# Transposing the first two row tiles before their 1/std is known, with the scale applied when V leaves PSUM

## The chip, the cores and the metric

The kernel runs on one core of one Trainium2 chip. The metric is the device time of one launch in microseconds (us). Before the change the median of 4 runs is 693.38 us (693.23 to 695.09).

## The reference

x is 2048 rows of 1024 numbers in bf16. One transformer block is computed: attention with a causal window of 256 on a layer norm of x, then a feed-forward part with SiLU on a layer norm of the result. The layer norms have no learned scale or shift. What matters here is the head of it:

```
def _layernorm(x, axis=-1, eps=1e-5):
    m = jnp.mean(x, axis=axis, keepdims=True)
    v = jnp.var(x, axis=axis, keepdims=True)
    return (x - m) / jnp.sqrt(v + eps)
...
qkv = (x @ wqkv) ... ; q, k, v = qkv[0], qkv[1], qkv[2]
h  = x + _A_ref(_layernorm(x, axis=-1), A_wqkv, A_wo)
h2 = h + _B_ref(_layernorm(h, axis=-1), B_w1, B_w2)
```

Each row of V is (row of x − mean) / std times the V columns of wqkv. The division by std is one number for each row, so it can be done before the product or after it.

## The kernel before

The 2048 rows are 4 blocks of 512, and each block is 4 row tiles of 128 rows. A product needs the normed rows transposed, so that the 1024 columns lie on the 128 partitions in 8 slices (kt 0 to 7). `lnT_b[0]` holds the transposed block 0: 8 slices by 512 rows.

Block 0 is the start of the program, when nothing else can run yet. Its V product has 8 groups: row tile j (0 to 3) by column half c (0, 1). `v_group(0, j, c)` is 8 matmuls of 128x512 (one for each kt) into one bank of PSUM (the matmul's output memory), and a copy of that bank into `v`. The matmuls have line L245 and the copy L247. The Q and K products of block 0 follow (`qk_group`, L255, copied by L257), which need all four row tiles of `lnT_b[0]`. Two banks take turns for these groups (`acc_banks`, `next_acc`).

The order of the work is written by hand: each engine's queue holds its instructions in the order in which the program emits them, and an instruction that waits holds up those behind it on the same engine. The order on each queue before the change:

- SP's queue issues loads: x tile 0, the first half of the V weights (`load_wqkv(2 * D)`, 1 MB, L139), x tile 2, the second half of the V weights, x tile 3, and the first Q weights. Tile 1 is issued from ScalarE's queue. Later come one DMA transpose (`ln_transpose`, L198) for tile 3, three more weight loads, and the four x tiles of block 1.
- TensorE (PE) first runs 11 matmuls on zeros to be warm (L162). Tiles 0, 1 and 2 are transposed on PE (`turn_first`, two 128x128 transposes at a time, L223) and copied from PSUM to `lnT_b[0]` by ScalarE (L224). Tile 3 goes through the DMA transpose.
- The layer norm of a tile: VectorE (DVE) reads it twice for statistics (`ln_half`, L166, then L174), ScalarE takes the root (`ln_root`, L201), DVE the reciprocal (L208) and the norm itself (`ln_norm`, L194). For tiles 0 and 1 the norm is done in quarters inside `ln_first`, one quarter of tile 0 on ScalarE (L217).
- V groups run in the order (j, c) = (0,0), (1,0), (0,1), (1,1), (2,0), (2,1), (3,0), (3,1).

During block 0's 16 Q and K groups, the layer norm of block 1 is given out as 16 steps (4 statistics, 4 steps of 1/std, 4 norms, 4 DMA transposes), none after each of the first 4 groups, one after each of the next 6, and two after each later one. Block 1's V product starts after them, with the first attention scores of block 0 (L360) in front. The odd groups among the 16 are copied out by DVE, the even ones by ScalarE.

Of the kernel before, what the change touches and what calls it, by code (L numbers as in the profile page):

```python
# [9 lines left out]
F32 = mybir.dt.float32  # L10
I32 = mybir.dt.int32
ACT = mybir.ActivationFunctionType
ALU = mybir.AluOpType

P = 128
# [29 lines left out]
def kernel(  # L45
# [10 lines left out]
    nc = tc.nc  # L56
# [3 lines left out]
    S, D = x2d.shape  # L60
# [4 lines left out]
    KT = D // P  # L65
# [4 lines left out]
    scale = float(DH) ** -0.5  # L70

    const = ctx.enter_context(tc.tile_pool(name="const", bufs=1))
    small = ctx.enter_context(tc.tile_pool(name="small", bufs=2))
# [12 lines left out]
    r_e = big.tile([P, 13312], BF16, name="r_e")  # L86
# [4 lines left out]
    tp_ps = [tp_pool.tile([P, 1024], BF16, name=f"tp{i}") for i in range(4)]  # L91
    o_ps = [ps.tile([P, 8, 64], F32, name=f"o_ps{i}") for i in range(2)]
    acc_ps = [ps.tile([P, 512], F32, name=f"acc{i}") for i in range(2)]

    def view(region, off, *dims):
        n = 1
        for d in dims:
            n *= d
        ap = region[:, off:off + n]
        if len(dims) == 2:  # L100
            return ap.rearrange("p (a b) -> p a b", b=dims[1])
        if len(dims) == 3:
            return ap.rearrange("p (a b c) -> p a b c", b=dims[1], c=dims[2])
        return ap
# [4 lines left out]
    lnT_b = [view(r_w, 24576, KT, 512), view(r_t, 0, KT, 512)]  # L109
    x_ring = [view(r_o, i * 1024, 1024) for i in range(8)]  # L110
# [17 lines left out]
    wqkv_v = A_wqkv.rearrange("(kt p) n -> p kt n", p=P)  # L128
# [5 lines left out]
    def load_x(b, j, queue=nc.sync):  # L134
        queue.dma_start(out=x_ring[(b % 2) * 4 + j], in_=x2d[(b * 4 + j) * P:(b * 4 + j + 1) * P, :])  # L135

    def load_wqkv(c0):
        dst = wqk[:, :, c0:c0 + 512] if c0 < 2 * D else wv[:, :, c0 - 2 * D:c0 - 2 * D + 512]
        nc.sync.dma_start(out=dst, in_=wqkv_v[:, :, c0:c0 + 512])  # L139

    eps = const.tile([P, 1], F32, name="eps")
    nc.vector.memset(eps[:], LN_EPS)
# [1 line left out]
    nc.scalar.activation(out=dummy[:], in_=eps[:], func=ACT.Sqrt)  # L144

    load_x(0, 0)
    load_wqkv(2 * D)
    load_x(0, 1, nc.scalar)
    load_x(0, 2)
    load_wqkv(2 * D + 512)  # L150
    load_x(0, 3)
    load_wqkv(0)

    ident = const.tile([P, P], BF16, name="ident")
    make_identity(nc, ident[:])
    warm = view(r_e, 0, 2, 512)
    nc.vector.memset(warm, 0.0)
    nc.gpsimd.memset(v[:, :, :, DH:VW], 1.0)


    for i in range(11):
        nc.tensor.matmul(o_ps[i % 2][:].rearrange("p a b -> p (a b)"), lhsT=warm[:, 0, 0:P], rhs=warm[:, 0, :], start=True, stop=True)  # L162


    def ln_half(xt, stats, c):
        nc.vector.bn_stats(out=stats[:, c, :], in_=xt[:, c * 512:(c + 1) * 512])  # L166

    def ln_stats(xt, st, j, half_done=None):
        stats = half_done
        if stats is None:  # L170
            stats = small.tile([P, 2, 6], F32, name="ln_st", tag="ln_st")
            ln_half(xt, stats, 0)
        ln_half(xt, stats, 1)
        nc.vector.bn_aggr(out=st[:, j, :], in_=stats[:])  # L174
# [18 lines left out]
    def ln_norm(xt, st, rs, j):  # L193
        nc.vector.tensor_scalar(out=xt, in0=xt, scalar1=st[:, j, 0:1], scalar2=rs[:, j:j + 1],  # L194
                                op0=ALU.subtract, op1=ALU.mult)

    def ln_transpose(xt, dst, j):
        nc.sync.dma_start_transpose(out=dst[:, :, j * P:(j + 1) * P], in_=xt)  # L198

    def ln_root(st, rs, j):  # L200
        nc.scalar.activation(out=rs[:, j:j + 1], in_=st[:, j, 1:2], func=ACT.Sqrt, bias=eps[:], scale=1.0)  # L201

    def ln_first(xt, st, rs, j, parts, on_act=0):

        if on_act:
            shift = small.tile([P, 2], F32, name="ln_shift", tag="ln_shift")
            nc.scalar.activation(out=shift[:, 0:1], in_=st[:, j, 0:1], func=ACT.Identity, scale=-1.0)
        nc.vector.reciprocal(out=rs[:, j:j + 1], in_=rs[:, j:j + 1])  # L208
        if on_act:
            nc.scalar.activation(out=shift[:, 1:2], in_=shift[:, 0:1], func=ACT.Identity, scale=rs[:, j:j + 1])  # L210
        n = 1024 // parts
        for h in range(parts):
            part = xt[:, h * n:(h + 1) * n]
            if h < parts - on_act:
                ln_norm(part, st, rs, j)
            else:
                nc.scalar.activation(out=part, in_=part, func=ACT.Identity, bias=shift[:, 1:2], scale=rs[:, j:j + 1])  # L217

    def turn_first(j, h):

        for i in range(2):
            kt = h * 2 + i
            nc.tensor.transpose(out=tp_ps[h][:, i * P:(i + 1) * P], in_=x_ring[j][:, kt * P:(kt + 1) * P], identity=ident[:])  # L223
        nc.scalar.copy(out=lnT_b[0][:, h * 2:(h + 1) * 2, j * P:(j + 1) * P],  # L224
                       in_=tp_ps[h][:, 0:256].rearrange("p (k q) -> p k q", q=P))

    def ln_tiles(tag):
        st = small.tile([P, 4, 2], F32, name=f"st_{tag}", tag=f"st_{tag}")
        rs = small.tile([P, 4], F32, name=f"rs_{tag}", tag=f"rs_{tag}")
        return st, rs  # L230
# [3 lines left out]
    acc_banks = list(a[:] for a in acc_ps)  # L234

    def next_acc():
        acc_n[0] += 1
        return acc_banks[acc_n[0] % len(acc_banks)]

    def v_group(b, j, c, copy, between=None):  # L240
        acc = next_acc()
        for kt in range(KT):
            if between:
                between(kt)
            nc.tensor.matmul(acc, lhsT=lnT_b[b % 2][:, kt, j * P:(j + 1) * P], rhs=wv[:, kt, c * 512:(c + 1) * 512],  # L245
                             start=(kt == 0), stop=(kt == KT - 1))
        copy(out=v[:, b * 4 + j, c * 16:(c + 1) * 16, 0:DH], in_=acc.rearrange("p (h d) -> p h d", d=DH))  # L247
# [172 lines left out]
    class Stream:  # L420
# [18 lines left out]
        def between(self, kt):  # L439
            if self.seen * self.n >= self.done * 192:  # L440
                self.bursts[self.done]()
                self.done += 1
            if self.seen * self.n * 2 >= (self.given * 2 + 1) * 192:
                if pending:
                    pending.pop(0)()
                coming.append(self.pieces[self.given])
                if len(coming) > self.behind:
                    pending.append(coming.pop(0))
                self.given += 1
            self.seen += 1  # L450

    dve, act = nc.vector.tensor_copy, nc.scalar.copy


    st, rs = ln_tiles("a")
    half = small.tile([P, 2, 6], F32, name="ln_st", tag="ln_st")
    ln_stats(x_ring[0], st, 0)
    ln_root(st, rs, 0)
    ln_half(x_ring[1], half, 0)
    ln_first(x_ring[0], st, rs, 0, 4, 1)  # L460
    ln_stats(x_ring[1], st, 1, half)
    for h in range(4):
        turn_first(0, h)
        if h == 2:
            ln_root(st, rs, 1)
    ln_first(x_ring[1], st, rs, 1, 4)
    ln_stats(x_ring[2], st, 2)

    held = []

    def turn_1(kt):
        if kt == 7:
            turn_first(1, 0)

    def turn_1_rest(kt):
        if kt == 2:
            turn_first(1, 3)
            act(**held.pop())
            ln_root(st, rs, 2)

    v_group(0, 0, 0, lambda **args: held.append(args), turn_1)
    turn_first(1, 1)
    turn_first(1, 2)
    v_group(0, 1, 0, act, turn_1_rest)
    ln_first(x_ring[2], st, rs, 2, 1)
    ln_stats(x_ring[3], st, 3)
    ln_root(st, rs, 3)
    ln_first(x_ring[3], st, rs, 3, 1)
    ln_transpose(x_ring[3], lnT_b[0], 3)
    for c0 in (D, 512, D + 512):  # L490
        load_wqkv(c0)
    v_group(0, 0, 1, act)
    for h in range(4):
        turn_first(2, h)
    v_group(0, 1, 1, act)
    v_group(0, 2, 0, act)
    v_group(0, 2, 1, act)
    nc.scalar.activation(out=dummy[:], in_=eps[:], func=ACT.Exp)
    v_group(0, 3, 0, act)
    v_group(0, 3, 1, act)  # L500

    ps_tp.__exit__(None, None, None)
    ps_sc = tc.tile_pool(name="ps_sc", bufs=1, space=bass.MemoryType.PSUM, reuse_waits="tile")
# [28 lines left out]
    for g0 in range(0, G, 4):  # L532
        for w in range(2):
            for g in range(g0, g0 + 4):
                qk_group(0, w, g, dve if g % 2 else act)
                n = g0 * 2 + w * 4 + g % 4
                for _ in range(0 if n < 4 else 1 if n < 10 else 2):
                    if steps:
                        steps.pop(0)()
    assert not steps  # L540
# [101 lines left out]
    for b in range(NB):  # L642
# [4 lines left out]
        for ft in range(FT):  # L647
# [8 lines left out]
            if b == 0 and 6 <= ft < 14:  # L656
                j, c = divmod(ft - 6, 2)
# [10 lines left out]
        for j in range(4):  # L668
# [9 lines left out]
            for acc, (c0, c1) in zip(accs, cols):  # L678
                mm2(acc, j, c0, c1, early, FT)
                nc.vector.scalar_tensor_tensor(out=t_out[j % 2][:, c0:c1], in0=acc[:, 0:c1 - c0], scalar=0.5,  # L680
                                               in1=t_in[j % 2][:, c0:c1], op0=ALU.mult, op1=ALU.add)
# [36 lines left out]
```

The softmax here doesn't subtract the row's maximum and nothing guards it: scores larger than these inputs give would overflow.

## Time and profile before

One profiled execution was traced. Its own time is beside its span here, and all times below are from the start of that span.

| | us |
|---|---|
| median of 4 runs | 693.38 |
| profiled execution: device time | 693.34 |
| its span, first to last instruction | 691.4 |
| around the span | 1.9 |
| PE busy | 686.0 (99%) |
| DVE, ScalarE, GpSimd busy | 290.9, 241.9, 160.9 |
| first x tile landed (DVE starts on it) | 4.19 |
| first V matmul | 7.87 |
| first Q/K matmul in the chain | 22.93 |
| first V matmul of block 1 in the chain | 50.91 |

A line of a timeline reads: start, duration, engine, line of the program, operation, output<-input with shapes, how many, and in brackets how long the engine had been idle and what ended it. DMA issues appear with the suffix "q" (SPq is SyncE's queue), and the duration there is that of the issue, not of the transfer. A DMA answer gives the size and the time from the start of the issue to landing. A chain line gives start, duration and what the end of the program depended on at that time.

### The profile page before, as it was taken

To read this page: it belongs to the slowest core of one execution; us is meant where nothing else is said; L and a number is where in the kernel's file an instruction comes from. 1 tells how busy PE (TensorE), PEld (TensorE's weight loads), DVE (VectorE), ACT (ScalarE), POOL (GpSimd) and SP (SyncE) were. 2 spreads that over 40 slices of the span, in tenths; PEclk is the share of its full clock that TensorE was granted. 3 is DMA by queue.
4 is the path that set the end of the run, shared out by engine and by line. 5 is a ranking of instruction groups with operands and counts; after the bars stand their busy time and mean duration, and the time that the engine had idled before them with its cause. 6 is when DMAs were issued, how large, how long until landed. Compare 5 with 4: busy or idle time off the path is not lost.

```text
span 691.4 us, 14223 instructions
## 1 busy us (share of the span) xinstructions
PE 686.0 (99%) x6011; PEld 331.5 (48%) x6011; DVE 290.9 (42%) x609; ACT 241.9 (35%) x463; POOL 160.9 (23%) x295
## 2 busy tenths in 40 slices
PE   8999999999999999999999999999999999999998
PEld 3444455555555555544444444444444444444445
DVE  5267646744444439534315133343133251333111
ACT  5326666766666666421310033300133100233000
POOL 1007666656666666500000000000000000000000
PEclk9999999999999999999999999999999999999999
DMA  7732241136240889971023410032300024100110
GB/s 251 250 55 78 39 82 59 26 59 188 72 131 17 241 235 276 226 269 49 13 79 111 94 39 0 1 91 69 85 0 1 19 93 95 39 1 1 30 39 24
DMA packets 76463, 60.95 MB, mean 88 GB/s; under 512 B 50288, under 2 KB 60528, under 8 KB 76400
## 3 DMA queue, kind: packets, MB, share of 16 engines
q1 hardware_dynamic: 76256, 59.78, 32.1%
q8 instruction: 47, 0.77, 0.5%
q10 hardware_dynamic: 144, 0.26, 0.1%
q14 instruction: 16, 0.13, 0.1%
HBM read 39.85 MB, written 8.39 MB: 70 GB/s over the span
## 4 chain that ended last, share of the span: by engine, by line
PE 98%; DMA 1%; SPq 0%; DVE 0%; issue 0%
PE hacc L628 19%; PE hacc L665 18%; PE acc L255 17%; PE acc L665 10%; PE acc L628 9%; PE acc L245 8%; PE acc L276 7%; PE o_ps L388 5%; PE sc L308 3%; PE hacc L276 1%; DMA r_w<-in_A_wqkv_dram 1%; PE sc L360 1%; PE sc L334 1%; PE tp L223 0%; SPq L135 0%; DVE r_t L680 0%
## 5 line engine op out<-in xcount | busy, mean ns | idle before, releaser
L378 POOL TENSOR_SCALAR_AFFINE_SELECT r_e<-r_e 128x512 bf16<-128x512 bf16 (+1 forms) x288 | 157.9, 563 | 126.1 <-ACT r_e L368 62.5
L665 PEld LDWEIGHTS <-r_a 128*128 128x128 bf16 x952 | 90.9, 98 | 103.0
L628 PEld LDWEIGHTS <-r_w 128*128 128x128 bf16 x896 | 87.4, 98 | 105.2 <-issue 0.4
L665 PE MATMUL hacc<-r_a 128*128 128x512 bf16 (+2 forms) x616 | 122.5, 360 | 0.0
L628 PE MATMUL hacc<-r_e,r_w 128*128 128x512 bf16 x456 | 100.9, 379 | 0.0
L320 ACT ACTIVATE r_e<-sc 128x768 bf16<-128x768 f32 x96 | 78.2, 814 | 48.3 <-PE sc L308 48.3
L637 ACT ACTIVATE r_n<-hacc 128x512 f32<-128x512 f32 x30 | 17.9, 597 | 178.9 <-PE hacc L628 178.9
L665 PE MATMUL acc<-r_a 128*128 128x512 bf16 x336 | 74.0, 379 | 0.0
L255 PEld LDWEIGHTS <-r_w 128*128 128x128 bf16 x512 | 44.2, 97 | 46.1 <-issue 1.0
L255 PE MATMUL acc<-r_t,r_w 128*128 128x512 bf16 x256 | 63.4, 379 | 0.0
L257 DVE CAST r_a<-acc 128x512 bf16<-128x512 f32 x56 | 38.6, 690 | 56.5 <-PE acc L255 56.4
L255 PE MATMUL acc<-r_w 128*128 128x512 bf16 x256 | 59.9, 379 | 0.0
L388 PEld LDWEIGHTS <-r_e 128*128 128x128 bf16 x1440 | 47.4, 96 | 17.9
L276 PE MATMUL acc<-r_o,r_a 128*128 128x512 bf16 x208 | 51.9, 379 | 0.0
L628 PE MATMUL acc<-r_e,r_w 128*128 128x512 bf16 x216 | 49.1, 379 | 0.0
L388 PE MATMUL o_ps<-r_a,r_e 128*128 128x33 bf16 x1440 | 48.1, 178 | 0.0
L680 DVE SCALAR_TENSOR_TENSOR r_t<-hacc,r_t 128x512 bf16<-128x512 f32 (+2 forms) x22 | 14.0, 635 | 56.3 <-PE hacc L665 56.3
L321 ACT ACTIVATE r_e<-sc 128x256 bf16<-128x256 f32 x96 | 37.4, 390 | 0.0
L680 DVE SCALAR_TENSOR_TENSOR r_t<-acc,r_t 128x512 bf16<-128x512 f32 x12 | 8.3, 692 | 64.2 <-PE acc L665 64.2
L638 DVE SCALAR_TENSOR_TENSOR r_a<-r_n,hacc 128x512 bf16<-128x512 f32 x30 | 20.7, 688 | 33.0 <-ACT r_n L637 33.0
L628 PE MATMUL hacc<-r_a,r_w 128*128 128x512 bf16 x144 | 32.9, 379 | 0.0
L276 PEld LDWEIGHTS <-r_a 128*128 128x128 bf16 x256 | 21.8, 97 | 22.3
(79 smaller groups left out, 534.9 us busy)
## 6 DMA issues: line engine op xcount, KB each, us to landing
r_w<-in_B_w_dram SPq DMA_DIRECT2D x8, 896.0 KB, 5.4
r_a<-in_B_w_dram SPq DMA_DIRECT2D x7, 1024.0 KB, 7.6
r_w<-in_A_wqkv_dram SPq DMA_DIRECT2D x6, 1024.0 KB, 9.2
h_dram<-r_t SPq DMA_DIRECT2D x16, 256.0 KB, 3.2
r_t<-h_dram SPq DMA_DIRECT2D x16, 256.0 KB, 2.8
out_dram<-r_t SPq DMA_DIRECT2D x31, 128.0 KB, 1.7
r_o<-in_A_x_dram SPq DMA_DIRECT2D x15, 256.0 KB, 4.0
r_e<-h_dram SPq DMA_DIRECT2D x3, 1024.0 KB, 5.8
```

What stands on the lines that cost most here:

```text
L245: nc.tensor.matmul(acc, lhsT=lnT_b[b % 2][:, kt, j * P:(j + 1) * P], rhs=wv[:, kt, c * 512:(c + 1) * 512], start=(kt == 0), stop=(kt == KT ...
L255: nc.tensor.matmul(acc, lhsT=wqk[:, kt, col0:col0 + P], rhs=lnT_b[b % 2][:, kt, :], start=(kt == 0), stop=(kt == KT - 1))
L257: copy(out=(qT, kT)[which][b][:, g, :], in_=acc)
L276: nc.tensor.matmul(acc, lhsT=qT[b][:, g, j * P:(j + 1) * P], rhs=wo[:, g, c * 512:(c + 1) * 512], start=(g == 0), stop=(g == G - 1))
L308: nc.tensor.matmul(sc[hh // 2][half * 64:half * 64 + 64, hh % 2, col:col + qb - qa], lhsT=kT[t // 4][r0:r0 + DH, g, k0:k0 + 64], rhs=qT[b] ...
L320: nc.scalar.activation(out=tri[:, :, :, 64:256], in_=both, func=ACT.Exp, scale=scale)
L321: nc.scalar.activation(out=e[:, 1024:1280].rearrange("p (h q) -> p h q", q=P), in_=bank[:, :, 192:320], func=ACT.Exp, scale=scale)
L378: nc.gpsimd.affine_select(out=dst, in_=src, pattern=[[0, n] for n in dst.shape[1:-1]] + [[sgn, P]], compare_op=ALU.is_ge if upper else ALU ...
L388: nc.tensor.matmul(o_ps[pair][:, qt * 2 + hh, 0:VW], lhsT=chunk_of(i, bank, piece, pair, hh), rhs=v[:, b * 4 + kt, g * 4 + pair * 2 + hh, ...
L628: nc.tensor.matmul(acc, lhsT=w1[:, kt, ft * P:(ft + 1) * P], rhs=ln2T[b][:, kt, :], start=(kt == 0), stop=(kt == KT - 1))
L665: nc.tensor.matmul(acc[:, 0:c1 - c0], lhsT=gT[:, ft, j * P:(j + 1) * P], rhs=w2[ft // 4][:, ft % 4, c0:c1], start=(ft == 0), stop=(ft == F ...
L680: nc.vector.scalar_tensor_tensor(out=t_out[j % 2][:, c0:c1], in0=acc[:, 0:c1 - c0], scalar=0.5, in1=t_in[j % 2][:, c0:c1], op0=ALU.mult, o ...
```

## The change

Row tiles 0 and 1 are transposed for V with only the mean taken off; 1/std is applied when V leaves PSUM. Q and K still need the normed tile, so tiles 0 and 1 are normed afterwards in place and transposed a second time by DMA, over the centred ones.

- The zeros for the warm-up shrink to 128 columns, read four times by a stride of 0, and are written first; the warm-up has 9 matmuls in place of 11.
- Load order on SP: x0, x1, V weights half 0 in two DMAs of 512 KB (kt 0 to 3, kt 4 to 7), x2, half 1 in two DMAs, x3, Q weights. ScalarE issues no load.
- The mean of tile 0 comes half from a ScalarE pass with an accumulated sum and half from a DVE statistics pass; that of tile 1 from a ScalarE pass over 1024 columns. DVE takes the mean off in quarters into a new place.
- The variances of tiles 0 and 1 come from a `Square` pass on ScalarE over 1024 columns each.
- Four PSUM banks take turns for block 0's V groups, and the first four groups stay there until their 1/std is known. Tile 2's transposes come after group (1,1), straight in front of group (2,0).
- The DMA transposes are three (tiles 0, 3, 1) in place of one, ahead of the three weight loads.
- Block 1's layer norm steps start after 6 of the 16 Q and K groups in place of 4.

```
-    load_wqkv(2 * D)
-    load_x(0, 1, nc.scalar)
+    load_x(0, 1)
+    load_wqkv(2 * D, 2)
     load_x(0, 2)
-    load_wqkv(2 * D + 512)
+    load_wqkv(2 * D + 512, 2)
     load_x(0, 3)
     load_wqkv(0)
...
-    for i in range(11):
+    for i in range(9):
...
+    def mean_first():
+        nc.scalar.activation(out=scrap[:, 0:512], in_=x_ring[0][:, 512:1024], func=ACT.Identity, scale=-1.0 / D, accum_out=mean[:, 0:1])
+        ln_half(x_ring[0], half, 0)
+        nc.vector.tensor_scalar(out=mean[:, 1:2], in0=half[:, 0, 1:2], scalar1=half[:, 0, 4:5], scalar2=-0.25, op0=ALU.add, op1=ALU.mult)
+        nc.scalar.activation(out=scrap, in_=x_ring[1], func=ACT.Identity, scale=-1.0 / D, accum_out=mean[:, 3:4])
+    def center(j):
+        for h in range(4):
+            out, in0 = (x[j][:, h * 256:(h + 1) * 256] for x in (x_mid, x_ring))
...
+    def hold(**args):
+        held.append(args)
+    def scaled(j):
+        args = held.pop(0)
+        nc.scalar.activation(func=ACT.Identity, scale=rs[:, j:j + 1], **args)
+    def place(at):
+        return lambda kt: turn_first(*at[kt], x_mid[at[kt][0]]) if kt in at else None
+    acc_banks += [o[:].rearrange("p a b -> p (a b)") for o in o_ps]
+    def var_first(j):
+        nc.scalar.activation(out=scrap, in_=x_ring[j], func=ACT.Square, bias=mean[:, j + 2:j + 3], scale=1.0, accum_out=var[:, j:j + 1])
+    def root_first(j):
+        nc.scalar.activation(out=rs[:, j:j + 1], in_=var[:, j:j + 1], func=ACT.Sqrt, bias=eps[:], scale=1.0 / D)
+    def norm_first(j):
+        nc.vector.tensor_scalar(out=x_ring[j], in0=x_ring[j], scalar1=mean[:, j + 2:j + 3], scalar2=rs[:, j:j + 1], op0=ALU.add, op1=ALU.mult)
+    mean_first()
+    center(0)
+    center(1)
+    nc.vector.tensor_tensor(out=mean[:, 2:3], in0=mean[:, 0:1], in1=mean[:, 1:2], op=ALU.add)
+    turn_first(0, 0, x_mid[0])
+    turn_first(0, 1, x_mid[0])
+    v_group(0, 0, 0, hold, place({1: (0, 2), 3: (0, 3), 5: (1, 0), 6: (1, 1), 7: (1, 2)}))
+    turn_first(1, 3, x_mid[1])
+    var_first(0)
+    ln_stats(x_ring[2], st, 2)
+    ln_root(st, rs, 2)
+    root_first(0)
+    var_first(1)
+    root_first(1)
+    ln_recip(rs, 2)
+    ln_norm(x_ring[2], st, rs, 2)
+    ln_recip(rs, 0)
+    norm_first(0)
+    v_group(0, 1, 0, hold)
+    v_group(0, 0, 1, hold)
+    scaled(0)
+    ln_stats(x_ring[3], st, 3)
+    ln_recip(rs, 1)
+    scaled(1)
+    ln_root(st, rs, 3)
+    norm_first(1)
+    v_group(0, 1, 1, hold)
     for h in range(4):
+        turn_first(2, h, x_ring[2])
+    ln_recip(rs, 3)
+    ln_norm(x_ring[3], st, rs, 3)
+    scaled(0)
+    scaled(1)
+    for j in (0, 3, 1):
+        ln_transpose(x_ring[j], lnT_b[0], j)
     for c0 in (D, 512, D + 512):
         load_wqkv(c0)
...
-                for _ in range(0 if n < 4 else 1 if n < 10 else 2):
+                for _ in range(0 if n < 6 else 1 if n < 10 else 2):
```

More of the change, by code (lines that the diff above doesn't have):

```diff
@@ L135, in load_x, with load_wqkv @@
         queue.dma_start(out=x_ring[(b % 2) * 4 + j], in_=x2d[(b * 4 + j) * P:(b * 4 + j + 1) * P, :])
-    def load_wqkv(c0):
+    def load_wqkv(c0, parts=1):
         dst = wqk[:, :, c0:c0 + 512] if c0 < 2 * D else wv[:, :, c0 - 2 * D:c0 - 2 * D + 512]
-        nc.sync.dma_start(out=dst, in_=wqkv_v[:, :, c0:c0 + 512])
+        n = KT // parts
+        for k in range(0, KT, n):
+            nc.sync.dma_start(out=dst[:, k:k + n, :], in_=wqkv_v[:, k:k + n, c0:c0 + 512])
+    warm = view(r_e, 0, P)
+    nc.vector.memset(warm, 0.0)
     eps = const.tile([P, 1], F32, name="eps")
@@ L155 @@
     make_identity(nc, ident[:])
-    warm = view(r_e, 0, 2, 512)
-    nc.vector.memset(warm, 0.0)
     nc.gpsimd.memset(v[:, :, :, DH:VW], 1.0)
-    for i in range(11):
-        nc.tensor.matmul(o_ps[i % 2][:].rearrange("p a b -> p (a b)"), lhsT=warm[:, 0, 0:P], rhs=warm[:, 0, :], start=True, stop=True)
+    wide = bass.AP(tensor=warm.tensor, offset=warm.offset, ap=[warm.ap[0], [0, 4], warm.ap[1]])
+    for i in range(9):
+        nc.tensor.matmul(o_ps[i % 2][:].rearrange("p (a c) b -> p a (c b)", c=2), lhsT=warm, rhs=wide, start=True, stop=True)
     def ln_half(xt, stats, c):
@@ L201, in ln_root, with ln_recip, turn_first @@
         nc.scalar.activation(out=rs[:, j:j + 1], in_=st[:, j, 1:2], func=ACT.Sqrt, bias=eps[:], scale=1.0)
[L203 to L207, printed above, removed]
+    def ln_recip(rs, j):
         nc.vector.reciprocal(out=rs[:, j:j + 1], in_=rs[:, j:j + 1])
[L209 to L219, printed above, removed]
+    def turn_first(j, h, src):
         for i in range(2):
             kt = h * 2 + i
-            nc.tensor.transpose(out=tp_ps[h][:, i * P:(i + 1) * P], in_=x_ring[j][:, kt * P:(kt + 1) * P], identity=ident[:])
+            nc.tensor.transpose(out=tp_ps[h][:, i * P:(i + 1) * P], in_=src[:, kt * P:(kt + 1) * P], identity=ident[:])
         nc.scalar.copy(out=lnT_b[0][:, h * 2:(h + 1) * 2, j * P:(j + 1) * P],
@@ L455 @@
     st, rs = ln_tiles("a")
[L456 to L461, printed above, removed]
-    for h in range(4):
[L463 to L489, printed above, removed]
+    x_mid = [view(r_e, 1024 + 1024 * j, 1024) for j in range(2)]
@@ new lines @@
+    scrap = view(r_e, 3072, 1024)
+    mean = small.tile([P, 4], F32, name="mean")
+    var = small.tile([P, 2], F32, name="var")
+    half = small.tile([P, 2, 6], F32, name="ln_half")
+    def mean_first():
[3 more added lines that the diff above has]
+        nc.scalar.activation(out=scrap, in_=x_ring[1], func=ACT.Identity, scale=-1.0 / D, accum_out=mean[:, 3:4])
@@ new lines, in center @@
+    def center(j):
+        for h in range(4):
+            out, in0 = (x[j][:, h * 256:(h + 1) * 256] for x in (x_mid, x_ring))
+            if j == 0:
+                nc.vector.tensor_scalar(out=out, in0=in0, scalar1=mean[:, 0:1], scalar2=mean[:, 1:2], op0=ALU.add, op1=ALU.add)
+            else:
+                nc.vector.tensor_scalar(out=out, in0=in0, scalar1=mean[:, 3:4], scalar2=None, op0=ALU.add)
+    held = []
+    def hold(**args):
[3 more added lines that the diff above has]
+        nc.scalar.activation(func=ACT.Identity, scale=rs[:, j:j + 1], **args)
@@ L491 @@
         load_wqkv(c0)
[L492 to L495, printed above, removed]
     v_group(0, 2, 0, act)
@@ L500 @@
     v_group(0, 3, 1, act)
+    del acc_banks[2:]
     ps_tp.__exit__(None, None, None)
```

## The prediction

> **What bounds the kernel now.** I read the page first: PE is busy for 686.0 of 691.4 us. So only the start, before PE has dense work, and stalls between groups can give anything. The chain of waits over the first 30 us says what the start hangs on:
>
> ```profile
> 1.26 6.57 DMA r_w<-in_A_wqkv_dram
> 10.83 3.02 PE acc L245 x14
> 14.30 8.63 PE acc L245 x40
> 22.93 7.12 PE acc L255 x33
> ```
>
> The first V weights land at 7.83. Then PE works through to Q and K at 22.93. A matmul in the run of 40 takes 8.63 / 40 = 0.216 us, so V's 64 need 13.81; from 7.87 to 22.93 are 15.06. The 16 transposes in that stretch of the chain take 0.89 (0.11 + 0.22 + 0.11 + 0.45). Only 0.36 is stall. Group (3,0) starts 16 matmuls before 22.93, at 19.48.
>
> Next the timeline of the other engines from 10 to 24 us, for tile 3, the last tile that V needs:
>
> ```profile
> 12.62 1.28 DVE L166 BATCH_NORM_STATS2 ln_st<-r_o 128x6 f32<-128x512 bf16 x2
> 13.93 0.21 DVE L174 BATCH_NORM_AGGREGATE st_a<-ln_st 128x2 f32<-128x12 f32 x1
> 14.17 0.29 ACT L201 ACTIVATE rs_a<-st_a,eps 128x1 f32<-128x1 f32 x1 [1.43 <-DVE st_a L174]
> 14.50 0.17 DVE L208 RECIPROCAL rs_a<-rs_a 128x1 f32<-128x1 f32 x1 [0.36 <-ACT rs_a L201]
> 14.70 0.55 DVE L194 TENSOR_SCALAR r_o<-r_o,st_a,rs_a 128x1024 bf16<-128x1024 bf16 x1
> 15.28 1.32 SPq L198 DMA_TRANSPOSE r_w<-r_o  x1
> ```
>
> The transpose is issued at 15.28, 1.11 us after its root started. DMA answers for the issues in flight at 3 to 4 us (x3, issued at 3.16), at 16 to 17 (tile 3's transpose), and at 44 to 45 (the first of block 1's four transposes) add the landings:
>
> ```profile
> r_o<-in_A_x_dram SPq DMA_DIRECT2D x1, 256.0 KB, 9.0
> ```
> ```profile
> r_w<-r_o SPq DMA_TRANSPOSE x1, 3.2
> ```
> ```profile
> r_t<-r_o SPq DMA_TRANSPOSE x1, 4.8
> ```
>
> x3 lands at 3.16 + 9.0 = 12.16. Tile 3 is transposed at 15.28 + 3.2 = 18.48, 1.0 us before PE wants it. This margin is what the change spends.
>
> **The change part by part.**
>
> Front. Windows show 344 to 383 GB/s from 3 to 14 us, whatever is queued, so bytes set the landings. Weights' kt 4 to 7 still have x0, x1 and 1 MB in front of their end: 7.83, as now. Kt 0 to 3 lack 0.52 MB of that, 1.4 us at 370 GB/s: about 6.3. On that point the Trainium skill speaks against the halves: "DMA: Bandwidth & Descriptors", Rules for kernel authors, wants 1 MiB or more in a DMA and small ones joined. No gap shows here between the 256 KB x loads and the 1 MB ones, so I charge nothing. If each extra DMA paid in series the 2 us that the page fits for GpSimd's DMAs, the forecast would be some 2 us worse, an estimate.
>
> First transposes. DVE had x0 at 4.19. One half of statistics (0.64), a small DVE op (0.15) and one quarter (0.34) give about 5.4 in place of 6.78. But ScalarE must run the pass over x1 before the first copy. Its price comes from two groups of the page:
>
> ```profile
> L320 ACT ACTIVATE r_e<-sc 128x768 bf16<-128x768 f32 x96 | 78.2, 814 | 48.3 <-PE sc L308 48.3
> L321 ACT ACTIVATE r_e<-sc 128x256 bf16<-128x256 f32 x96 | 37.4, 390 | 0.0
> ```
>
> 512 columns more cost 0.42, so 1024 cost 1.03 and 512 cost 0.60. A sum for each row appears nowhere in this trace: between nothing and one more small ScalarE instruction (0.30, L210); I take 0.2. First pass 4.2 to 5.0, second 5.0 to 6.2, first copy (0.35) to 6.55: V starts at about 6.55, not 7.87. Four matmuls and the last four transposes of tile 0 are done by 7.7; then kt 4 waits for its weights until 7.87. The gain so far is 4 matmuls, 0.86, and with the 0.36 of stall at most 1.22 us.
>
> Middle. From 7.87: four matmuls and tile 1's eight transposes end at 9.3, and the last copy at 9.77. Group (0,1) needs weights that landed at 2.35 + 9.2 = 11.55; its kt 4 starts at 11.76. Group (1,1) ends at 14.36. All its evictions are held in four banks, so no copy stands in the way; with two it would.
>
> The chain to tile 3, in order of each queue, is where the gain goes:
> - ScalarE starts the `Square` pass of tile 0 behind that copy, at 9.67: 1.03, 0.10 for a bias read from memory (L201 0.29 against L207 0.19), 0.2 for the sum: 11.0.
> - Tile 2's root stands behind it, to 11.25. DVE needs it: reciprocal, norm of tile 2 (0.55), reciprocal and norm of tile 0 (0.55) end at 12.72.
> - Statistics of tile 3 overlap that end by 0.08 and take 1.52 (12.62 to 14.14 above): 12.64 to 14.16. x3 itself would allow 12.2.
> - Reciprocal of tile 1, 14.24; ScalarE waits for it with the second eviction `scaled(1)`: 0.59 (L247) + 0.10, from 14.3 to 15.0. Tile 3's root is queued behind: start 14.9. Before it was 14.17.
> - 1.11 later SP issues tile 3's transpose: 16.01. Landing +3.2, and 0.05: group (3,0) at 19.25.
>
> The PE side is earlier: tile 2's copies are behind that root too, the first ends at 15.47, so PE idles from 14.81 to 15.5, and would reach group (3,0) at 18.97. So tile 3 ends last: 19.25 against 19.48, **0.23 us gained**; the rest of 1.22 goes into these waits.
>
> Bounds: with x3 as the limit (12.2) and no cost for the sums, the issue is at 15.6 and the gain 0.65. With sums at 0.3 the gain is 0.1. For the transposes' lag, several rows: 3.2 alone, 3.2 for both of a pair at 387, 4.4 and 3.9 for a pair at 85, 4.8 for the first of four. Tile 3's now has tile 1's directly behind it, a pair with nothing else in flight, like that at 387: I take 3.2 and keep 4.4 for the range.
>
> Moved and added behind that. SP issues two transposes more (2 x 1.32) ahead of the weights: the first of these lands near 18.7 + 5.8 = 24.5, and is wanted after four Q groups, 22.7 + 6.9 = 29.6. Tile 1's transpose lands at 17.4 + 3.2 = 20.6, before 22.7. x of block 1 lands at about 33 (traffic ended at 30.3, plus some 2.5); its statistics, two groups later, start after 33.5. These cost nothing. The later norms put block 1's first norm behind six 1/std ops (1.18) after the DVE copy that ends at 44.3, so the first transpose issues at 46.06 in place of 44.86; with the lag of 4.8 it lands at 50.86, and block 1's V matmul starts at 50.91. Nothing, with 0.05 to spare; 0 to 0.3 if not.
>
> Warm-up. The first weight loads on PE come every 0.43 us (1.96, 2.38, 2.81 ...), the V matmuls every 0.216. The spacing shortened about 5.0, 3.5 us after the start. Nine at 0.43 are 3.9 us from about 1.1: enough. By the skill ("TensorE: Matmul & The Clock Gate", Part 1) the clock is freed after a busy window of about 3.4 us whose start is not tied to the program; 3.9 us then leaves less room than the 4.3 of now for a whole one.
>
> Sum: 693.34 − 0.23 = **693.1** for the profiled execution, which stands 0.04 under the median of the runs.
>
> **Rivals.**
> - Lean chain: sums cost nothing and x3 alone limits. 693.34 − 0.65 = 692.7. For: DVE waits for x3 from 12.16 at best. Against: the pass over squares alone ends at 10.8. 13%.
> - Slower: tile 3's transpose takes longer because it is one of three. Place: DMA, between 16.0 and group (3,0). It decides from a lag of 3.42. At 4.8, group (3,0) starts at 20.86, 1.4 late: 694.7; at 6.2 (the longest of all, at 278) 696.1. For: three of block 1's four took 4.3 to 4.8. Against: pairs at 387 and 79 stay near 3.2, and tile 0's transpose is 3 us ahead. 17%.
> - Slower: the clock is not yet freed when V starts. Eight matmuls at 0.43 add 1.7, less the wait for kt 4 (0.2): 1.5 on the chain to tile 3, 694.6. Against: the spacing above. 6%.
> - `Square` forces function tables to be loaded: two loads of 1.28 (L144) ahead of tile 2's root, 2.6 on the chain, 695.7. Against: Sqrt, Identity and copies alternate in the trace with no load between 2.1 and 20.1. 2%.
> - It doesn't advance V at all (ScalarE's pass late, V still at 7.87): the chain is set from 7.87 on anyway, so 0.2 at most: inside the forecast.
>
> **How the numbers follow.** 0.2%, 1.4 us, is about what a measurement of this kernel can tell from no change. The forecast has 55%, from 692.8 to 693.8. Nothing above gives 1.4 us gained; 4% are for a bound I missed, 3% for a loss I don't see. Over 1.4 lost: half of the transposes' rival, half of the clock's, the tables, and the unseen: 17%. The other 79% are within. The range, 692.5 to 694.8, leaves out the far ends of these.
>
> **What would show it.** V's first matmul near 6.5 and a short wait before its fifth; tile 3's root near 14.9 directly behind an eviction; its transpose issued near 16.0; PE idle near 15 and shortly before group (3,0), which starts near 19.25; the first Q matmul near 22.7. It is wrong if group (3,0) does not wait for the DMA, if the lag is over 3.5, if a table load stands between 3 and 19 us, or if block 1's V waits.

## The result and the profile after

The changed kernel takes 694.48 us in the median of 45 runs, the kernel before 693.44 in 67 runs on the same occasions; the ratio is 1.0012, 95% interval 1.0006 to 1.0018. The medians are 1.04 us apart, and by the ratio the change loses about 0.8 us (0.12%). That is under the 0.2% that the prediction named, but it is a loss where a gain of 0.23 us was forecast. More striking is the scatter: 692.15 to 696.51, where all but six of the 67 runs of before lie between 693.0 and 694.0.

The granted clock (the share of full speed that TensorE was given, as a mean over the execution) parts the 45 runs into three heaps: 22 at 692.15 to 694.19 with 1.00 (one of them 0.999), 16 at 694.48 to 696.09 with 0.998, and seven at 696.09 to 696.51 with 1.00. The median is the fastest run of the second heap.

The profiled execution took 693.70, with a span of 692.0. The first fence is PE's timeline of it; the columns are start, duration, engine, line, operation, output<-input, how many, and idle time before.

```profile
1.05 4.02 PE L166 MATMUL o_ps<-r_e 128*128 128x512 bf16 x9 [1.05 <-DVE eps L147]
5.41 0.65 PE L214 MATMUL tp<-ident,r_e 128*128 128x128 bf16 x4 [0.34 <-DVE r_e L464]
6.27 0.61 PE L236 MATMUL acc<-r_w 128*128 128x512 bf16 x1 [0.21 <-ACT r_w L215]
6.67 0.42 PE L214 MATMUL tp<-ident,r_e 128*128 128x128 bf16 x2
6.89 1.06 PE L236 MATMUL acc<-r_w 128*128 128x512 bf16 x2
...
10.01 0.28 PE L214 MATMUL tp<-ident,r_e 128*128 128x128 bf16 x2
10.12 0.38 PE L236 MATMUL acc<-r_w 128*128 128x512 bf16 x1
10.34 0.28 PE L214 MATMUL tp<-ident,r_e 128*128 128x128 bf16 x2
10.45 3.62 PE L236 MATMUL o_ps<-r_w 128*128 128x512 bf16 x16
...
23.45 2.75 PE L246 MATMUL acc<-r_w 128*128 128x512 bf16 x12
```

V starts at 6.27, 1.6 us earlier than before, as the change intends. But two matmuls take 1.06 us there and two transposes 0.42. From 10.0 on two transposes take 0.28, and 16 matmuls 3.62. The chain of waits says it without the overlap of the ends, and shows the path to group (2,0):

```profile
7.09 0.85 PE acc L236 x2
...
10.92 1.24 ACT r_e L483 x2
12.16 0.20 ACT rs_a L205
...
13.79 1.21 DVE ln_st L170 x2
...
15.35 0.69 ACT r_a L475
16.04 0.18 ACT rs_a L205
16.22 0.27 ACT r_w L215
16.49 0.05 issue
16.53 1.90 PE acc L236 x8
18.43 3.45 PE o_ps L236 x16
...
23.61 27.63 PE acc L246 x128
```

Two matmuls take 0.85, that is 0.43 each; at the usual rate they take 0.43 together (3.45 for 16). The 9 warm-ups did not bring PE to full speed, and V's first group ran at half of it until about 10.0. What follows is the prediction's own chain, only later: the `Square` pass (L483, at 10.92 in place of 9.67), tile 2's root (L205), the statistics of tile 3 (L170), the second scaled eviction (L475), tile 3's root, tile 2's first copy (L215), group (2,0) (at 16.53 in place of 15.5).

That hardly anything later counts is seen from one sum. In every trace of this study, the device time less the start of the first Q/K matmul on PE's timeline is the same within 0.33 us; most of them are in the table:

| kernel, profiled execution | first Q/K matmul | device time | difference |
|---|---|---|---|
| before | 22.77 | 693.34 | 670.57 |
| changed | 23.45 | 693.70 | 670.25 |
| changed, three more traces | 25.03, 23.38, 23.47 | 695.30, 693.64, 693.85 | 670.27, 670.26, 670.38 |
| filled | 22.79 | 693.19 | 670.40 |
| filled and reordered | 22.18 | 692.43 | 670.25 |
| filled, one DMA for each weight half | 25.22 | 695.61 | 670.39 |
| before, 9 warm-ups | 23.86 | 694.35 | 670.49 |

So each trace can be read, to within these tenths, by what happens up to that matmul.

### The profile page after: what moved, and what is told of

It reads as the page before. It is cut to its first block, busy times and chain, and to the rows that moved or that the text cites. A ratio compares the mean times of both kernels' runs of the same rounds, so it can differ in the third digit from the quotient of the medians.

```text
span 692.0 us, 14232 instructions
## 1 busy us (share of the span) xinstructions
PE 687.3 (99%) x6009; PEld 332.0 (48%) x6009; DVE 289.4 (42%) x609; ACT 245.6 (35%) x468; POOL 161.0 (23%) x295
## 4 chain that ended last, share of the span: by engine, by line
PE 98%; ACT 1%; DMA 0%; DVE 0%; issue 0%; ACTq 0%
PE hacc L661 19%; PE hacc L698 17%; PE acc L246 17%; PE acc L698 10%; PE acc L661 9%; PE acc L236 7%; PE acc L267 7%; PE o_ps L379 5%; PE sc L299 3%; PE hacc L267 1%; PE sc L351 1%; PE sc L325 1%; PE o_ps L236 0%; DMA r_o<-in_A_x_dram 0%; ACT r_e L483 0%; DVE ln_st L170 0%
```

## The experiments

Two theories stood against each other. **C (clock):** the shortened warm-up, and the gaps in PE's work that the earlier front leaves, let V's first group run at half clock. **Q (queues):** the chain through ScalarE and DVE to tile 3 and tile 2's copies is the whole loss. Each timed kernel is compared with the kernel before on the same chip and the same occasion (693.20, 693.21 and 693.10 us on the three occasions).

### Nine warm-ups in the kernel before

```
-    for i in range(11):
+    for i in range(9):
```

> The kernel before with 9 warm-ups in place of 11, nothing else. Theory C: PE stops about 0.5 to 0.9 earlier and then idles until 6.78, so the clock often comes only after V has begun: median 693.8 to 695, and a spread of 2 us or more, though none of the change's other parts is there. Theory Q: 693.4 as before, with the same narrow spread.

694.50 in the median (693.09 to 694.84, 11 runs), ratio 1.0015 (1.0006 to 1.0023). This one edit costs as much as the whole change, though nothing else is in it. PE's timeline of the kernel before has these two lines:

```profile
1.55 4.31 PE L162 MATMUL o_ps<-r_e 128*128 128x512 bf16 x11 [1.55 <-DVE r_e L157]
...
7.87 1.67 PE L245 MATMUL acc<-r_w 128*128 128x512 bf16 x7 [0.16 <-DMA r_w<-in_A_wqkv_dram]
```

With 9 warm-ups:

```profile
1.55 4.02 PE L162 MATMUL o_ps<-r_e 128*128 128x512 bf16 x9 [1.55 <-DVE r_e L157]
6.71 1.12 PE L223 MATMUL tp<-ident,r_o 128*128 128x128 bf16 x8 [1.13 <-DVE r_o L194]
7.80 2.83 PE L245 MATMUL acc<-r_w 128*128 128x512 bf16 x7
```

PE stands idle for 1.13 in front of the transposes, and then 7 V matmuls take 2.83 where they took 1.67 with 11 warm-ups. C is right on this, and Q is out as the whole cause. The spread is 1.75, not the 2 that was expected.

### Eleven warm-ups in the changed kernel

```
-    for i in range(9):
+    for i in range(11):
```

> The changed kernel with 11 warm-up matmuls again in place of 9, nothing else. Theory C (clock): in the profile of the changed kernel the matmuls come every 0.43 us until about 10.0 and every 0.216 after it, so the 9 warm-ups did not free the clock and 14 of the first matmuls and transposes ran at half speed; the time of the changed kernel scatters from 692.2 to 696.5 with the moment at which the clock comes. With two more warm-ups (0.43 each) PE is busy until 5.75 and the gap to the first transpose at 5.41 is gone: median 692.4 to 693.3, and most runs under 693.5. Theory Q (queues: the chain through ScalarE and DVE to tile 3 is the whole cause, and the first matmuls would be no earlier with a free clock): unchanged, 694.2 to 694.8.

693.39 (692.46 to 695.47, 11 runs), ratio 1.0007 (0.9998 to 1.0015): a tenth above the range of C. Eight of the 11 runs lie under 693.7. The other three (694.44, 695.06, 695.47) have a mean granted clock of 0.998, and the trace is of one of them. Its PE timeline comes first, then two stretches of 1 us; their columns are the stretch and its length, each engine's busy time and instructions, and at the end the granted clock, the share of the DMA engines and GB/s:

```profile
1.05 3.89 PE L166 MATMUL o_ps<-r_e 128*128 128x512 bf16 x11 [1.05 <-DVE eps L147]
5.26 0.54 PE L214 MATMUL tp<-ident,r_e 128*128 128x128 bf16 x4 [0.32 <-DVE r_e L464]
7.13 0.54 PE L236 MATMUL acc<-r_w 128*128 128x512 bf16 x1 [1.33 <-DMA r_w<-in_A_wqkv_dram]
7.46 0.42 PE L214 MATMUL tp<-ident,r_e 128*128 128x128 bf16 x2
7.67 1.06 PE L236 MATMUL acc<-r_w 128*128 128x512 bf16 x2
```
```profile
7.00:8.00 1.00, 0.87 (x4) 0.46 (x4) 0.00 (x0) 0.09 (x1) 0.00 (x0) 0.61 1.05 354
...
10.00:11.00 1.00, 1.00 (x8) 0.57 (x6) 0.82 (x3) 0.69 (x2) 0.00 (x0) 0.69 1.08 394
```

The warm-ups were fast (11 in 3.89, where 9 took 4.02 above). Then PE waited 1.33 for the first part of the weights, which landed at 7.08, and V is at half speed again, for some 3.4 us. Half of that is 1.7 us, and 1.7 of 693 us is the 0.002 by which the mean clock falls short of 1. So the number of warm-ups is one part of the loss; the other is a gap in which the clock is lost once more. The interval of the ratio overlaps with that of the change (1.0006 to 1.0018), so it is the traces and the next runs that tell the two parts from each other.

### Three more traces of the changed kernel

No edit. The kernel was run again to catch other executions.

> The changed kernel as it is, for a second trace. Theory C: the time follows the moment at which PE's matmuls go from 0.43 to 0.216 us (10.0 in the first trace, 693.7): each us of V at 0.43 costs 0.5. A run near 692.3 has it before 6.3, one near 696.3 near 14 to 15, and one at clock 0.998 has fast warm-ups and a slow V. Theory Q: the times differ by waits on tile 3's transpose, with the same spacing of matmuls.

The second: 695.30. Stretches of its first 12 us, with the columns as above:

```profile
5.00:6.00 1.00, 0.54 (x4) 0.32 (x5) 1.00 (x5) 0.99 (x4) 0.00 (x0) 1.00 0.91 224
6.00:7.00 1.00, 0.00 (x0) 0.00 (x0) 0.57 (x4) 0.00 (x0) 0.00 (x0) 1.00 1.02 327
7.00:8.00 1.00, 0.00 (x0) 0.00 (x0) 0.00 (x0) 0.00 (x0) 0.00 (x0) 0.91 1.06 333
8.00:9.00 1.00, 0.86 (x4) 0.46 (x4) 0.00 (x0) 0.03 (x1) 0.00 (x0) 0.50 1.03 353
...
11.00:12.00 1.00, 1.00 (x10) 0.51 (x9) 0.62 (x2) 0.79 (x3) 0.00 (x0) 0.88 1.08 388
```

PE has nothing to do from 5.55, because the first weights land only at 8.10 (1.73 + 6.37). The clock falls to a half at 7.82 (0.91 is 0.82 of a us at 1 and 0.18 at a half), and comes back at 11.24 (0.88 is 0.24 at a half and 0.76 at 1). This is the loss caught in the act, and the first Q/K matmul comes at 25.03.

> The changed kernel as it is, for a third trace; expected as for the second.

693.64. All as in the first trace: half speed from 6.32 to about 9.8, first Q/K matmul at 23.38.

> The changed kernel as it is, for a fourth trace; expected as for the second.

693.85: half speed from 6.39 to about 9.7, first Q/K matmul at 23.47. In these two the granted clock reads 1.00 in every stretch, while matmuls come every 0.43: a clock that has not yet been freed doesn't show in that number, and only the spacing of the matmuls shows it.

C holds in all four traces: three executions in which the clock had not come, one in which it came and went. None of the four is one of the quick executions near 692.3, and none is one of those at 696.1 to 696.5 with a clock of 1.00.

### Filling the gap

```
-    for i in range(9):
+    for i in range(10):
...
     turn_first(0, 1, x_mid[0])
+    for i in range(2):
+        nc.tensor.matmul(o_ps[i % 2]..., lhsT=warm, rhs=wide, start=True, stop=True)
```

> The changed kernel with 10 warm-ups in place of 9 and two more zero matmuls between the first four transposes and V's first matmul, where PE idles in its profile (5.85 to 6.27). Theory C: PE has no gap from 1.05 until V, so the clock is freed before or early in V in nearly every run: median 692.3 to 693.0, spread under 2 us between the fastest and all but a tenth of the runs. If it were the number of warm-ups alone and not the gaps, it would be no better than the kernel with 11 warm-ups. Theory Q: unchanged, 694.2 to 694.8.

693.29 (692.26 to 695.40, 11 runs), ratio 1.0002 (0.9993 to 1.0010). That is 0.3 above the expected range, but 10 of the 11 runs lie between 692.26 and 693.61, and nothing distinguishes it from the kernel before. The one at 695.40 has a clock of 0.998. PE's timeline:

```profile
5.21 0.39 PE L214 MATMUL tp<-ident,r_e 128*128 128x128 bf16 x4
5.44 0.59 PE L498 MATMUL o_ps<-r_e 128*128 128x512 bf16 x2
6.41 0.38 PE L236 MATMUL acc<-r_w 128*128 128x512 bf16 x1 [0.38 <-DMA r_w<-in_A_wqkv_dram]
...
7.28 0.38 PE L236 MATMUL acc<-r_w 128*128 128x512 bf16 x1
8.49 0.38 PE L236 MATMUL acc<-r_w 128*128 128x512 bf16 x1 [0.84 <-DMA r_w<-in_A_wqkv_dram]
```

V runs at full speed from its first matmul. Its fifth waits 0.84 for the weights' second part, which landed at 8.45 here; before, the whole half was there at 7.83. With the clock repaired in most runs, what is left of the change is what the prediction said: about nothing.

### The weights' halves in one DMA

```
-    load_wqkv(2 * D, 2)
+    load_wqkv(2 * D)
...
-    load_wqkv(2 * D + 512, 2)
+    load_wqkv(2 * D + 512)
```

in the filled kernel.

> The filled kernel (10 warm-ups, two zero matmuls) with each half of the V weights in one DMA of 1 MB again. V then starts when the whole first half has landed, 7.8 to 8.4, instead of starting early and stopping at its fifth matmul; the first four matmuls and four transposes (1.3) follow the landing. If the early start is worth what the prediction said (0.86 in front of the chain to tile 3): 0.9 to 1.3 slower than the filled kernel, 694.1 to 694.6, and PE idle before V, so a wider spread. If two DMAs land later than one, by 0.5 as the filled kernel's profile suggests (8.45 against 7.83): 0.3 to 0.8 slower only.

695.78 (695.40 to 697.06, 6 runs), ratio 1.0038 (1.0026 to 1.0050): 2.5 slower than the filled kernel, beyond both expectations. All six runs have a granted clock of 0.997 or 0.998.

```profile
5.49 0.59 PE L498 MATMUL o_ps<-r_e 128*128 128x512 bf16 x2
8.35 0.59 PE L236 MATMUL acc<-r_w 128*128 128x512 bf16 x1 [2.27 <-DMA r_w<-in_A_wqkv_dram]
8.73 0.42 PE L214 MATMUL tp<-ident,r_e 128*128 128x128 bf16 x2
8.95 1.06 PE L236 MATMUL acc<-r_w 128*128 128x512 bf16 x2
```
```profile
7.00:8.00 1.00, 0.00 (x0) 0.00 (x0) 0.00 (x0) 0.00 (x0) 0.00 (x0) 1.00 1.00 346
8.00:9.00 1.00, 0.65 (x4) 0.37 (x4) 0.04 (x1) 0.00 (x0) 0.00 (x0) 0.50 1.08 387
...
11.00:12.00 1.00, 1.00 (x10) 0.65 (x9) 0.00 (x0) 0.60 (x2) 0.00 (x0) 0.80 1.08 388
```

The weights land at 8.31 (1.73 + 6.58), and with 2.27 idle ahead of V the clock falls in the trace; by their granted clock it fell in all six runs. So the two DMAs, against which the prediction quoted a rule, are worth 2.5 us here: they bring V's start forward by some 2 us (8.35 against 6.41), and they keep PE's gap short. Why the 1 MB DMA lands later here than before (8.31 against 7.83) was not tested; x1 now stands in front of it on the same queue.

### The order on ScalarE

```
     scaled(0)
     ln_stats(x_ring[3], st, 3)
     ln_recip(rs, 1)
-    scaled(1)
     ln_root(st, rs, 3)
...
         turn_first(2, h, x_ring[2])
+    scaled(1)
```

in the changed kernel, with its 9 warm-ups.

> The changed kernel with tile 3's root on ScalarE ahead of the second scaled eviction, and that eviction behind tile 2's four copies; still 9 warm-ups. In the profile of the changed kernel the eviction (15.35 to 16.04) stands between tile 3's statistics (15.22) and its root, and PE waits for tile 2's first copy from 16.1 to 16.53. Theory C: it takes at most 0.6 from every run, the spread stays: median 693.8 to 694.3, slowest above 695.5. Theory Q: the chain was the loss, so the median falls to 693.4 or less and the fastest runs fall by 0.6 too.

693.31 (692.29 to 695.92, 12 runs), ratio 1.0009 (0.9998 to 1.0020). The runs fall into two heaps, seven at 692.29 to 693.65 and five at 695.00 to 695.92, so the median says little: it lies in the range of Q (693.4 or less), but by the size of the heaps. The ends say more: the slowest are still over 695.5, as C expected, and the fastest is no lower than that of the changed kernel (692.15), against Q. In the trace (693.65) tile 2's first copy starts as soon as its transposes are through, 0.02 after them, and PE stands for 0.13 in front of group (2,0) (its transposes end at 16.35) in place of 0.29. The chain:

```profile
15.91 0.13 PE tp L214 x2
16.03 0.02 issue
16.06 0.38 ACT r_w L215
...
16.48 1.90 PE acc L236 x8
```

### Both repairs

The filled kernel with this order.

> The changed kernel with both repairs: 10 warm-ups and two zero matmuls in the gap, and tile 3's root ahead of the second scaled eviction, which stands behind tile 2's copies. In the profile of the filled kernel PE waits 0.45 (15.43 to 15.87) before group (2,0) and its first 8 matmuls take 0.17 too long. Theory C + queues (the clock is the large loss, the ScalarE queue a small one): 0.3 to 0.6 under the filled kernel, median 692.6 to 693.0, and under the kernel before. If the front's gain is lost for good elsewhere (arrival of the weights): no better than the filled kernel, 693.2 to 693.4.

692.88 (692.23 to 694.34, 11 runs), ratio 0.9997 (0.9988 to 1.0005). That is 0.4 under the filled kernel, inside the expected 0.3 to 0.6, but the traces give the order less: group (2,0) starts 7.23 after V's fifth matmul here and 7.38 in the filled kernel, 0.15. Most of the rest between the two traces is the weights' second part, which landed at 7.98 in this one (692.43) and at 8.45 in that (693.19). The first Q/K matmul comes at 22.18, 0.6 before that of the kernel before.

### More zero matmuls

The kernel with both repairs, first with six in place of two:

```
-    for i in range(2):
+    for i in range(6):
```

> As the kernel with both repairs, but six zero matmuls in place of two in front of V. With a free clock they end at about 7.1, later than the weights' first half lands in some runs, and earlier than in others. Theory C: a run is lost when PE idles before V (the runs at clock 0.998); with six, PE has no idle stretch over 0.5 before V's fifth matmul waits, so no run is over 694.5, median 692.6 to 693.2. Rival: V's start is the path, and the four more zero matmuls (4 x 0.216) cost up to 0.86: median 693.3 to 693.8.

693.49 (692.34 to 693.69, 11 runs), ratio 0.9999 (0.9990 to 1.0007). No run is over 694.5, as C has it; the median is 0.6 above that with two, as the rival had it. In the trace the zero matmuls end at 7.6, and V starts 1.1 later than with two. In the traces the first Q/K matmul comes at 22.70 in place of 22.18, so cover for the clock has a price where it stands in front of the work; the intervals of the two ratios overlap.

Then with three, and one more in front of V's fifth matmul:

```
-    for i in range(2):
+    for i in range(3):
...
+            if kt == 4:
+                nc.tensor.matmul(o_ps[0]..., lhsT=warm, rhs=wide, start=True, stop=True)
```

> The kernel with both repairs, with three zero matmuls in place of two in front of V and one more in front of V's fifth matmul, where PE waits for the weights' second part (0.41 in the profile of the kernel with both repairs, 0.84 in that of the filled one). Theory C: no gap over 0.3 is left from 1.05 until V runs on its own, so the clock is free before 7.9 in every run and stays so: median 692.5 to 692.9, no run over 693.8, against 694.34 for the slowest with both repairs. Rival, that V's start is the path: 0.2 to 0.4 slower than with both repairs, 693.1 to 693.3.

692.89 (692.31 to 693.88, 11 runs), ratio 1.0000 (0.9991 to 1.0009). Median as expected, slowest 0.08 above the bound of C; no better than with both repairs within what 11 runs can tell. No version of the study is surely faster than the kernel before: the medians of the two best lie 0.2 to 0.3 under it, and their intervals hold 1. What the filling did change is the granted clock: 0.998 stands in none of the 33 runs with both repairs or more zeros, and in 20 of the 57 runs with 9 warm-ups and the gap left open (16 of 45 and 4 of 12).

### Block 1's norms later, alone

```
-                for _ in range(0 if n < 4 else 1 if n < 10 else 2):
+                for _ in range(0 if n < 6 else 1 if n < 10 else 2):
```

in the kernel before.

> The kernel before with block 1's layer norm steps from the seventh of the 16 Q and K groups on, in place of the fifth; nothing else. The prediction costs this at nothing with 0.05 us to spare: 693.1 to 693.4, as before. Rival: block 1's first V matmul waits for its transpose, 0.3 or more, seen as a DMA wait near 51 us.

693.15 (692.89 to 693.46, 11 runs), ratio 0.9998 (0.9990 to 1.0007). No wait near 51 us: the edit is free, as predicted.

## Why the prediction was wrong, point by point

**The step that failed is the warm-up:** "Nine at 0.43 are 3.9 us from about 1.1: enough." It was not: in the first trace V's first group runs at half speed until about 10.0, and 9 warm-ups alone cost the kernel before 1.3 us (694.50 against 693.20). The prediction also took the clock, once freed, for kept, and put the idle time between the warm-up and V at nothing. In the second trace PE idled 2.59 there and the clock fell for 3.4 us. Each of the three traces with a granted clock of 0.998 shows such a fall and none with 1.00 does; 16 of the 45 runs have 0.998.

The prediction had half of this as a rival, a clock not yet freed when V starts, with 6% and 694.6. It gave the row that spoke against it too much weight: the spacing in one execution shortened after 3.5 us of work, but one execution shows one moment of the clock, not how the moment moves from run to run. That the median of 694.48 lies so near 694.6 is in part luck. The three traces of exactly that case took 693.64 to 693.85, 0.5 to 0.8 above the forecast and not 1.5; the median is as high as it is because 23 of the 45 runs belong to the two slower heaps, which that rival doesn't have.

The rule of the Trainium skill that the prediction cited beside its warm-up ("TensorE: Matmul & The Clock Gate", Part 1), a window not tied to the program, was the better guide. The runs agree with it: with the same start, the warm-ups reached full speed before 4.8 in one execution (9 in 3.76) and not at all in three (9 in 4.02 each).

**Where the gain of the front went.** The steps behind the clock can be checked on the filled kernel, whose fifth V matmul starts at 8.49. Counted from there: the `Square` pass at 1.78 (predicted 1.80), tile 3's statistics at 4.55 (4.77), its root at 6.78 (7.03), group (2,0) at 7.38 (7.63). The chain was right within 0.25. The time is 0.09 above the kernel before in place of 0.23 below, a difference that 11 runs can hardly tell from none; the term that differs in the traces is the landing of the weights' second part, taken as 7.83 and found at 8.45, 7.98 and 7.93 in three of them. For the first part 7.83 less 1.4 is 6.4, not the 6.3 that the prediction writes; nothing rests on it there, as V's start was put at 6.55.

**What held.** ScalarE's timeline of the changed kernel has the prices:

```profile
10.92 1.15 ACT L483 ACTIVATE r_e<-r_o,mean 128x1024 bf16<-128x1024 bf16 x1
11.97 0.19 ACT L483 ACTIVATION_READ_ACCUMULATOR r_e<-r_o,mean 128x1 f32 x1
12.06 0.28 ACT L205 ACTIVATE rs_a<-st_a,eps 128x1 f32<-128x1 f32 x1
...
15.35 0.69 ACT L475 ACTIVATE r_a<-o_ps,rs_a 128x512 bf16<-128x512 f32 x1 [0.77 <-DVE rs_a L208]
15.93 0.28 ACT L205 ACTIVATE rs_a<-st_a,eps 128x1 f32<-128x1 f32 x1
```

The sum is an instruction of its own, 0.19 (taken as 0.2); the pass over squares 1.15 (1.13); the scaled eviction 0.69 (0.69), with tile 3's root directly behind it. No table is loaded, so that rival falls. The rival on the transposes falls too: tile 3's took less than the 3.2 of the forecast, as the DMA answer for the issues at 17 to 18 us has it.

```profile
r_w<-r_o SPq DMA_TRANSPOSE x1, 2.8
```

It lands near 19.8, before PE wants group (3,0) at 20.16. So PE's side and not tile 3 set the end, by some tenths: the prediction had them 0.28 apart the other way round, and had named this as a sign of being wrong ("if group (3,0) does not wait for the DMA").

**The direction and the range.** A small gain was forecast and a small loss came. 692.5 to 694.8 holds the median, but the executions reach beyond both ends: the prediction never asked how far they would differ among themselves, 4.4 us here.

**What stays open.** Seven of the 45 runs lie at 696.09 to 696.51 with a granted clock of 1.00. By the sum of the table their first Q/K matmul comes near 26, 2.6 after that of the first trace; as each us at half speed loses half a us, V would have to stay at it until about 15 (an estimate). No trace caught one, so it isn't shown that the clock is the cause there; no run of the filled kernels with two DMAs lies above 694.34 with a clock of 1.00. Nor did a trace catch one of the quick runs near 692.3. Nor is it known why the first weights land at 8.10 in one execution of the changed kernel and at 6.1 to 6.4 in the three others.

## What to carry to other kernels

Work that comes earlier can lose its gain if PE is not at full clock when it comes: price a front by the rate at which PE will run it, and count every gap ahead of it, not only the first start. A warm-up that suffices in one trace may not in the next; look at the scatter of the runs and at the spacing of the matmuls, not at one profile. And when each engine's queue is in order, follow the new waits along each queue to the next thing that PE needs: here they ate what was left.

## What the runs showed of the hardware

- The clock falls fast. With 11 warm-ups PE was idle from 5.80 to 7.13 and the clock went to a half at 7.22; with whole DMAs it was idle from 6.08 and the clock went at 8.0; in the second trace from 5.55, and at 7.82. So 1.3 us without work was enough once. Shorter gaps were not: PE idled 0.91 ahead of the transposes in the kernel before and 0.84 ahead of V's fifth matmul in the filled one, and ran at full speed behind them. The times of the falls are worked out from the clock's mean over stretches of 1 us: 0.61 from 7 to 8 us is 0.22 at 1 and 0.78 at a half.
- It stayed at a half for 3.4 us each time: 7.22 to 10.62, 8.0 to 11.4, 7.82 to 11.24, with PE busy for nearly all of it. At half speed that is up to 1.7 us lost for one gap. The Trainium skill ("TensorE: Matmul & The Clock Gate", Part 1) gives a window of about 3.4 us, which agrees; it lets the clock fall after an idle window of that length, and here it fell after less idle time than that, so the measurement decides.
- Matmuls on zeros free this clock: PE had run nothing else when 11 of them took 4.31 in the kernel before and 3.89 in the changed one, where at 0.43 each they would take 4.9.
